# Unshifted exponentials with a checked range and a second, shifted program behind a branch; finishing in steps, like work kept together, B further ahead

## The chip, the cores and the metric

One core of a Trainium2 chip. Times are device microseconds (us) of a whole execution; most executions of one kernel agree within 0.3%. All runs told here were in the fast, undisturbed state, and each was timed beside runs of the kernel before on the same chip. The granted clock is the share of TensorE's full clock that the trace records, as a mean over the run.

## The reference, cut to what matters

Two independent blocks share the kernel: A, an attention over all 2,048 positions, and B, a causal attention in four segments of 512 with a memory carried from one segment to the next. Both have 32 heads of 32 columns. Their outputs stand side by side.

```python
# A
scores = einsum('bhqd,bhkd->bhqk', q, k) * 32 ** -0.5
o_A    = softmax(scores) @ v                  # 32 heads, 2048 x 2048
out_A  = o_A @ wo
# B, for each of four segments
p      = softmax(qs @ ks.T * scale + mask)    # 512 x 512, causal
a_mem  = (phi(qs) @ M) / (phi(qs) @ z + 1e-6)
o      = g * a_mem + (1 - g) * (p @ vs)
M, z   = M + phi(ks).T @ vs, z + phi(ks).sum()
out_B  = o @ wo
```

With the inputs given, scores are small: sums of 2,048 exponentials are near 2,048, so a softmax without a shift is safe here. Nothing guarantees that for other inputs.

## The kernel before

A Python planner writes the program: it keeps a simple clock for every engine, decides what TensorE does next, and records the operations. Each engine gets its list in the order recorded, and semaphores hold an operation back until what it needs is done.

Four heads are packed into the 128 rows of TensorE for the scores and into its columns for the value products. An A unit is four heads and 256 queries; a B item is four heads and one segment. TensorE writes its results to PSUM, and the probabilities go from there through a ring of 20 slots in SBUF. The main parts, with cuts marked `# ...`:

```python
SLOTS = [(0, 1, 2), (3, 4)]      # PSUM banks of the scores, used by turns
RING, HIGH = 20, 12

# scores and exponential: 3 banks, then 2
R.op("PE", f, ..., w=[("ps", bk) for bk in banks[:n]], mode="R")      # tiled by rows
cb, ck = self.cbA[b][:, k:k + 1], ("cbA", b, k)                       # B: cbB
R.op("ACT", lambda e: e.activation(self.PT[:, s0:s0 + n, 0:width], self.ps[...],
                                   ACTF.Exp, bias=cb, scale=SCALE), ..., cost=0.171 + n * width * 0.000833)

# the shift (B; A's is alike): squares, sums of squares, maximum over columns, over partitions
for k in range(2):
    R.op("DVE", lambda e, k=k: e.tensor_tensor(self.SQB[k][:, :], KQ[:, k, :], KQ[:, k, :], ALU.mult), ...)
R.op("PE", ...)                                    # 4 matmuls with blk32
yield from self.col_max(bank, 1, -SCALE, self.cbB[b][:, 0:1], ("cbB", b))   # reduce, diagonal, matmul, reduce
self.events.add(("sB", n))                         # only now may B's scores start

# value products and sums of one unit end: copy PSUM, then finish
R.op("DVE", lambda e: e.tensor_copy(self.OL[x][:, :], self.ps[:, OLB, :]), ...)
for q in range(2):                                 # finish()
    R.op("DVE", lambda e, Lq=Lq: e.reciprocal(Lq, Lq), ...)           # 128 columns each
    yield ("dve",)
R.op("DVE", lambda e: e.tensor_tensor(self.OTA[...], O, L, ALU.mult), ...)  # ...

# A or B next
it = b if b.kn < a.kn / 2 + LEAD else a            # LEAD = 3

# the planner's loop, when no scores can be put down now
full = len(self.ring_busy) > HIGH
for what in (("pv", "side") if full else ("side", "pv")):
    # "pv": a value product, if its exponentials are done
    # "side": projections, the memory, output projections, in chunks of up to 8 matmuls
```

## Time and profile before

| | before |
|---|---|
| median time (3 runs) | 1349.19 us (1347.47 to 1351.28) |
| score exponentials | 992, holding ScalarE 1,156 us |
| ScalarE's work, all activations (estimate from starts) | 1,191 us |
| ScalarE idle: first 160 us, middle, end | 67, 35, 58 us |
| TensorE's work (estimate, corrected below) | 1,203 us |
| changes of TensorE's tiling | 2,240 |

How the estimates are made: an activation's record is longer than what it holds of its engine, so I take starts. After an exponential of 1,024 elements the next one starts 996 ns later when nothing is waited for (median), after 1,536 elements 1,423 ns: 0.833 ns per element plus 143 ns. What lies beyond that between two starts is idle; a wait counts where it ends.

The head of the profile's page: busy time, share and count of each engine.

```profile
span 1350.1 us, 37376 instructions
PE 1232.8 (91%) x16968; PEld 509.2 (38%) x17194; DVE 831.7 (62%) x1391; ACT 1206.6 (89%) x1037; POOL 113.9 (8%) x207
```

The view of the waits from 140 to 1280 us (who waited <- for whom: us in total, times, longest):

```profile
ACT PT L471 <- PE ps L454: 16.8, 21, 3.8
```

In that stretch ScalarE hardly waits. The timeline shows what follows it (start, us, engine, line, operation, count, [idle before <- releaser]):

```profile
1268.84 7.42 ACT L471 ACTIVATE PT<-ps,cbA 128x1536 bf16<-128x1536 f32 x6 [0.62 <-PE ps L454]
1280.69 5.24 ACT L471 ACTIVATE PT<-ps,cbB 128x1536 bf16<-128x1536 f32 x5 [4.43 <-PE ps L454]
1285.80 0.65 ACT L762 ACTIVATE E<-KQB 128x512 bf16<-128x512 bf16 x1
1318.01 5.25 ACT L471 ACTIVATE PT<-ps,cbB 128x1024 bf16<-128x1024 f32 x5 [31.56 <-PE ps L454]
...
1331.17 15.48 PE L594 MATMUL ps<-WoB,OTB 128*128 128x512 bf16 x62 [5.91 <-DVE OTB L565]
```

The last B item comes 31.56 us late, and B's last output projection then runs alone.

### The profile page before, as it was taken

The page shows a single profiled execution, that of the slowest core. Times are in us where ns is not written, and L with a number is a line of the kernel's source. Part 1 is how long each engine was busy: PE and PEld are TensorE (multiplying, and loading weights), DVE is VectorE, ACT ScalarE, POOL GpSimd, SP SyncE. Part 2 cuts the span into 40 slices and gives each one's busy share as a digit, 9 for nine tenths or more (in the row PEclk, how much of TensorE's full clock was granted, in tenths as well). Part 3 has the DMA queues.
Part 4 walks back from the last instruction along what each step waited for, and adds up shares of the span by engine and source line. Part 5 has one row for each costly group of instructions (what it writes and reads, how often), then busy time and mean ns, then how long its engine had stood idle before and what let it go on. Part 6 is the DMA issues. An engine that isn't in the chain of part 4 may idle for free.

```text
span 1350.1 us, 37376 instructions
## 1 busy us (share of the span) xinstructions
PE 1232.8 (91%) x16968; PEld 509.2 (38%) x17194; DVE 831.7 (62%) x1391; ACT 1206.6 (89%) x1037; POOL 113.9 (8%) x207
## 2 busy tenths in 40 slices
PE   6788999999999988999899999999998999999996
PEld 3433343333333333333333333333333333333442
DVE  3665456555675567656647754757566675567674
ACT  3358989999999999999999999999999999999811
POOL 1000000100011011101100010111011111011110
PEclk9889999999999998999999999999998999999998
DMA  7325122311211122112211112111210113111111
GB/s 211 63 59 130 25 41 62 74 37 25 64 37 33 21 56 37 29 29 60 49 40 30 33 25 58 31 37 30 49 32 21 37 29 96 44 30 43 53 59 47
DMA packets 195870, 66.39 MB, mean 49 GB/s; under 512 B 187008, under 2 KB 187008, under 8 KB 195712
## 3 DMA queue, kind: packets, MB, share of 16 engines
q1 hardware_dynamic: 195712, 63.99, 20.2%
q8 instruction: 135, 2.21, 0.7%
q14 instruction: 23, 0.19, 0.0%
HBM read 40.90 MB, written 8.39 MB: 37 GB/s over the span
## 4 chain that ended last, share of the span: by engine, by line
ACT 66%; PE 23%; DVE 5%; SPq 2%; DMA 2%; issue 1%; POOL 0%; DVEq 0%
ACT PT L471 65%; PE ps L594 13%; PE ps L454 5%; PE ps L520 5%; DVE OL L540 2%; SPq L335 2%; ACT E L762 1%; DVE OL L530 1%; DMA PKt<-PH 1%; DVE outsb L837 1%; DMA WB<-in_B_wk_dram 0%; DMA out_dram<-outsb 0%; SPq L305 0%; DVE SQB L604 0%; DVE KQB L604 0%
## 5 line engine op out<-in xcount | busy, mean ns | idle before, releaser
L471 ACT ACTIVATE PT<-ps,cbA 128x1024 bf16<-128x1024 f32 (+1 forms) x832 | 1013.1, 1365 | 25.1 <-PE ps L454 24.6
L454 PE MATMUL ps<-QA,KA 32*128 32x256 bf16 x4096 | 328.7, 275 | 32.3 <-ACT PT L471 21.0
L520 PE MATMUL ps<-PT,ones 128*32 128x256 bf16 (+1 forms) x4864 | 315.0, 274 | 0.0
L520 PE MATMUL ps<-PT,VA 128*32 128x256 bf16 x4096 | 274.7, 282 | 1.5 <-DVE OL L530 0.8
L540 DVE RECIPROCAL OL<-OL 128x128 f32<-128x128 f32 x256 | 242.3, 948 | 5.2
L471 ACT ACTIVATE PT<-ps,cbB 128x768 bf16<-128x768 f32 (+3 forms) x160 | 171.4, 1197 | 62.5 <-PE ps L454 61.5
L454 PEld LDWEIGHTS ps<-QA,KA 32*128 32x128 bf16 x4096 | 95.3, 92 | 302.3 <-ACT PT L471 249.9
L594 PE MATMUL ps<-xB,WB 128*128 128x512 bf16 x683 | 187.2, 393 | 23.6 <-issue 13.2
L594 PE MATMUL ps<-xA,WA 128*128 128x512 bf16 x679 | 181.0, 385 | 14.1 <-issue 12.7
L491 POOL TENSOR_SCALAR_AFFINE_SELECT PT<-PT 128x512 bf16<-128x512 bf16 (+2 forms) x143 | 83.8, 601 | 1097.7 <-ACT PT L471 1096.5
L520 PEld LDWEIGHTS ps<-PT,VA 128*32 128x32 bf16 x4096 | 107.9, 95 | 134.3 <-issue 125.7
L530 DVE COPY OL<-ps 128x512 f32<-128x512 f32 x128 | 86.6, 677 | 73.6 <-PE ps L520 73.2
L520 PEld LDWEIGHTS ps<-PT,ones 128*32 128x32 bf16 x4864 | 130.7, 97 | 2.7 <-issue 0.3
L594 PEld LDWEIGHTS ps<-xB,WB 128*128 128x128 bf16 x768 | 62.4, 99 | 97.2 <-issue 45.0
L594 PEld LDWEIGHTS ps<-xA,WA 128*128 128x128 bf16 x768 | 61.5, 98 | 84.8 <-issue 34.7
L788 DVE RECIPROCAL den<-den 128x128 f32<-128x128 f32 x96 | 91.1, 949 | 2.1
L604 DVE CAST KQB<-ps 128x512 bf16<-128x512 f32 x64 | 43.4, 679 | 70.8 <-PE ps L594 70.8
L594 PE MATMUL ps<-WoB,OTB 128*128 128x512 bf16 x237 | 62.5, 391 | 8.8 <-DVE OTB L565 5.9
L837 DVE CAST outsb<-ps 128x512 bf16<-128x512 f32 x64 | 43.2, 678 | 37.9 <-PE ps L594 32.4
L454 PE MATMUL ps<-KQB 32*128 32x256 bf16 (+1 forms) x768 | 58.3, 265 | 6.9 <-ACT PT L471 4.3
L604 DVE CAST VT<-ps 128x512 bf16<-128x512 f32 x32 | 21.8, 681 | 67.3 <-PE ps L594 67.3
L594 PE MATMUL ps<-xA,OTA 128*128 128x512 bf16 x242 | 58.6, 380 | 3.7 <-issue 2.0
(76 smaller groups left out, 677.7 us busy)
## 6 DMA issues: line engine op xcount, KB each, us to landing
WB<-in_B_wk_dram SPq DMA_DIRECT2D x32, 256.0 KB, 2.8
WB<-in_B_wq_dram SPq DMA_DIRECT2D x32, 256.0 KB, 2.9
WB<-in_B_wv_dram SPq DMA_DIRECT2D x32, 256.0 KB, 3.1
out_dram<-outsb SPq DMA_DIRECT2D x32, 256.0 KB, 2.0
WA<-in_A_wqkv_dram SPq DMA_DIRECT2D x24, 256.0 KB, 3.6
OTA<-in_A_x_dram SPq DMA_DIRECT2D x16, 256.0 KB, 5.2
WoB<-in_B_wo_dram SPq DMA_DIRECT2D x1, 2048.0 KB, 9.8
xA<-in_A_wo_dram SPq DMA_DIRECT2D x1, 2048.0 KB, 9.4
```

What stands on the lines that cost most here:

```text
L335: R.dma(lambda e: e.dma_start(dst, src), w=keys, issue=0.5)
L454: ins = e.matmul(o, l, r, start=True, stop=True)
L471: op = R.op("ACT", lambda e: e.activation(self.PT[:, s0:s0 + n, 0:width], self.ps[:, banks[0]:banks[0] + n, 0:width], ACTF.Exp, bias=cb, s ...
L491: mo = R.op("POOL", lambda e, ap=ap, pat=pat: e.affine_select(ap, ap, pattern=pat, compare_op=ALU.is_ge, fill=0.0, base=0, channel_multipl ...
L520: ins = e.matmul(o, l, r, start=start, stop=end, skip_group_check=True)
L530: R.op("DVE", lambda e: e.tensor_copy(self.OL[x][:, :], self.ps[:, OLB, :]), r=[("ps", OLB)], w=[("OL", x)], cost=0.66)
L540: R.op("DVE", lambda e, Lq=Lq: e.reciprocal(Lq, Lq), r=[k], w=[k], cost=0.87)
L594: ins = e.matmul(o, l, rh, start=a, stop=z)
L604: op = self.R.op("DVE", lambda e: e.tensor_copy(dst, self.ps[:, bank, :]), r=[("ps", bank)], w=[dkey], cost=0.66)
L762: ex = R.op("ACT", lambda e: e.activation(self.E[:, k0:k1, :], KQ[:, k0:k1, :], ACTF.Exp), r=[("KQB", b, k) for k in range(k0, k1)], w=["E ...
L788: R.op("DVE", lambda e, cs=cs: e.reciprocal(self.den[:, cs], self.den[:, cs]), r=["den"], w=["den"], cost=0.9)
L837: op = R.op("DVE", lambda e, ns=ns, bank=bank, ob=ob: e.tensor_copy(self.outsb[ob][:, ns], self.ps[:, bank, :]), r=[("ps", bank)], w=[("ou ...
```

## The change

Its intent: exponentials without a shift, so that the bias is an immediate and the shift's work goes; a check on VectorE that sums and their reciprocals are in range, and the old, shifted program behind a branch if they aren't; the division split into steps between which other VectorE work may pass; TensorE stays with one kind of work once it has begun it; B is let further ahead of A.

```diff
-            cb, ck = self.cbA[b][:, k:k + 1], ("cbA", b, k)
+        cb, ck = 0.0, []                    # a pointer only if self.shifted
-                  cost=0.171 + n * width * 0.000833)
+                  cost=(0.171 if self.shifted else 0.085) + n * width * 0.000833)
@@ finish: a "dve" step before each reciprocal, and the check
-            R.op("DVE", lambda e, Lq=Lq: e.reciprocal(Lq, Lq), r=[k], w=[k], cost=0.87)
             yield ("dve",)
+            R.op("DVE", lambda e, cs=cs: e.reciprocal(rec[:, cs], L[:, cs]), r=[ko], w=[k], cost=0.93)
+        yield ("dve",)
+            R.op("DVE", lambda e: e.scalar_tensor_tensor(L, L, 1.0, rec, ALU.mult, ALU.add,
+                 accum_out=self.rng[:, u.seq:u.seq + 1]), ...)
@@ the shift: a_norm, total and B's part
+        if not self.shifted:
+            return
@@ pick
-            it = b if b.kn < a.kn / 2 + LEAD else a
+            it = b if b.kn < a.kn * SLOPE + LEAD else a        # SLOPE = 0.55
@@ the planner's loop
-            for what in (("pv", "side") if full else ("side", "pv")):
+            first = self.run if STICK and self.run else ("pv" if full else "side")
+            for what in (first, "side" if first == "pv" else "pv"):
...
+                if done:
+                    self.run = what                            # set to None by the next scores
@@ the end of each engine's program
+                eng.wait_ge(fast.sem["DVE"], fast.count[flag])
+                eng.reg_load(reg, self.flag[0:1, 0:1])
+                with eng.If_ne(reg, 0):
+                    fast.wait_all(eng)
+                    slow.play(eng, name)
```

Cut from it: the recorder's split into two programs, names of semaphores, the reduction of `rng` to one flag, a regrouping of scores that is switched off (`GROUP = 1`), the finishing tasks' higher priority, and a planned wait of a unit's first value product for the copy out of PSUM before it.

## The prediction

> **What bounds it now.** The groups view gives 992 score exponentials (PSUM to PT). In the timeline, starts of consecutive ones lie 996 ns apart after 1,024 elements and 1,423 after 1,536: 0.833 ns per element plus 143 ns. 1,216,512 elements and 992 instructions make 1,014 + 142 = 1,156 us; other activations add about 35. From 140 to 1280 us ScalarE waits for scores 16.8 us in all (view of the waits): it bounds that stage. The rest is a start of 140 us, where TensorE projects group 0 and ScalarE idles some 60 us, and a tail of 64 us after 1286 us: ScalarE waits 31.6 us for the last B item, then the last B output projection runs alone (62 matmuls recorded, 15.5 us).
>
> TensorE is close behind. From the starts of consecutive matmuls I estimate 1,160 us of work, 2,240 tiling changes at about 95 ns included, and 186 us of slack: 8 to 9% in the middle.
>
> **What changes.**
> 1. The bias becomes an immediate. The E exponentials have one already (reading SBUF) and hold ScalarE for stream + 93 ns. The Trainium skill, "ScalarE: Activation LUTs", section "What ACT_TABLE_LOAD costs", puts a [128,1] pointer operand at about 93 ns; no immediate exponential from PSUM is in the trace, so 143 - 93 = 50 ns is an estimate. Saved: 992 x 93 ns = 92 us, 80 of it where ScalarE bounds.
> 2. The shift's work goes: 64 + 128 square-sum and 51 diagonal matmuls (about 24 us of TensorE, plus some 18 us of tiling changes, estimated); on VectorE about 110 us.
> 3. Added on VectorE: 128 range checks of 256 float32; the like operation took 472 ns, so about 60 us. VectorE's total falls by 50 us (62% busy now, not binding).
> 4. Like work together: of 312 changes between value and full-array matmuls perhaps 120 vanish: 11 us of TensorE.
> 5. B ahead (0.55 for 0.5): B ends some six A units earlier. Each last A unit leaves TensorE about 5 us (estimate: 14.3 of ScalarE against 9 of TensorE), into which output projections fit: tail 64 to 25-35 us.
> 6. Finishing in steps lets evictions in between two reciprocals of 0.95 us: a few us at most.
> 7. At the end a reduction, a matmul, a register load and a jump over the second program: +5 us. Sums are near 2,048, so the flag stays 0.
>
> **Sum.** ScalarE's need: 1,190 - 92 = 1,098 us; TensorE's: 1,160 - 53 = 1,107: co-bound. ScalarE's idle time, 160 us now: start 85 to about 70 (no norm chain before the first scores), middle 17-25 to 28 (mutual waiting), tail 60 to about 28, end check 5. 1,098 + 70 + 28 + 28 + 5 = 1,229 us; predicted 1,228, range 1,192 to 1,260. Chances: faster by over 2% 0.97, within 0.02, slower 0.01.
>
> **What would show it.** (1) Exponentials start stream + 50 ns apart; if 90, the saving is half. (2) No square or diagonal matmuls, VectorE busy about 780 us. (3) Under 2,000 tiling changes; ScalarE's waits for scores in the middle grow from 17 to 30-50 us, TensorE's slack falls to 4-6%. (4) The last exponential is an A one, 25-35 us before the end. (5) About 5 us between last output and end.
>
> **What would make it wrong.** PSUM exponentials not gaining 93 ns (about 1,270); TensorE so full that preparation and output projections pile up at the end (1,250 or more); its granted clock (0.973 now) falling; VectorE queueing that holds PSUM; or a set flag, which runs everything twice.

## More of the kernel before

Groups by line and shape (line, engine, operation, tiles, shapes, count | busy us, mean ns | idle before, releaser):

```profile
L471 ACT ACTIVATE PT<-ps,cbA 128x1536 bf16<-128x1536 f32 x384 | 612.5, 1595 | 22.2 <-PE ps L454 22.1
L471 ACT ACTIVATE PT<-ps,cbA 128x1024 bf16<-128x1024 f32 x448 | 516.1, 1169 | 3.0 <-PE ps L454 2.5
...
L594 PE MATMUL ps<-xB,WB 128*128 128x512 bf16 x683 | 187.2, 393 | 23.6 <-issue 13.2 <-DMA WB<-in_B_wv_dram 4.3 <-DMA WB<-in_B_wk_dram 1.3
...
L594 PEld LDWEIGHTS ps<-xB,WB 128*128 128x128 bf16 x768 | 62.4, 99 | 97.2 <-issue 45.0 <-DMA WB<-in_B_wv_dram 4.8 <-DMA WB<-in_B_wk_dram 1.2
```

The first two lines are most of ScalarE's time; both read the bias from a tile (`cbA`). The last two hold a trap that I fell into: 768 weight loads, but 683 matmuls of the same line. The 85 others ran; they have no record. I come back to it.

"Middle" runs from 160 us to 30 us before the last exponential ends. TensorE's work is the time between its first and last matmul, less what the gaps between starts exceed the shortest gap of their kind by; it is good to some ten us.

## The result, and the profile after

The ratio of two kernels is the mean time of one's fast runs over that of the other's in the same rounds, so not quite the ratio of the medians quoted. Differences in us between kernels of different rounds are differences of such ratios times 1,350. The kernel before has a fourth run here, so its median differs from the one above.

| | before | after | predicted |
|---|---|---|---|
| median time | 1350.14 us | 1267.91 us (1265.81 to 1268.64) | 1228 (1192 to 1260) |
| ratio | 1 | 0.9391 (0.9372 to 0.9410) | |
| ScalarE's work | 1,191 us | 1,098 us | 1,098 us |
| ScalarE idle, first 160 us | 67 us | 71 us | 85 to 70 us |
| ScalarE idle, middle | 35 us | 59 us | 17-25 to 28 us |
| ScalarE idle, end (with the flag) | 58 us | 39 us | 60 to 33 us |
| TensorE's work, records corrected | 1,203 us | 1,161 us | 1,160 to 1,107 us |
| changes of tiling | 2,240 | 2,026 | under 2,000 |
| granted TensorE clock | 0.973 | 0.974 | |

The kernel became faster by 6.1%, 82 us, where 121 were predicted, and lies outside the range. Work and idle add up: 1,098 + 71 + 59 + 39 = 1,267 us. The prediction divided the 160 us of idle time before in another way (85, 17-25, 60) than the cuts used here do (67, 35, 58), so changes are safer to compare than levels: the start was to lose 15 us and gained 4, the middle was to gain 3 to 11 and gained 24, the end was to lose 27 and lost 19.

The page's head, and the groups:

```profile
span 1266.5 us, 36893 instructions
PE 1178.2 (93%) x16735; PEld 507.2 (40%) x16955; DVE 793.5 (63%) x1358; ACT 1119.8 (88%) x1037; POOL 115.1 (9%) x211
```

```profile
L532 ACT ACTIVATE PT<-ps 128x1536 bf16<-128x1536 f32 x416 | 625.7, 1504 | 47.6 <-PE ps L505 46.5
L532 ACT ACTIVATE PT<-ps 128x1024 bf16<-128x1024 f32 x480 | 508.3, 1081 | 16.1 <-PE ps L505 15.9
L674 PE MATMUL ps<-xB,WB 128*128 128x512 bf16 x696 | 186.9, 385 | 14.8 <-issue 10.2 <-DMA WB<-in_B_wv_dram 3.5 <-DMA WB<-in_B_wk_dram 0.4
...
L608 DVE SCALAR_TENSOR_TENSOR OL<-OL,SQ 128x256 f32<-128x256 f32 x128 | 57.4, 448 | 3.1
...
L608 DVE DVE_READ_ACCUMULATOR OL<-OL,SQ 128x1 f32 x128 | 10.4, 81 | 0.0
```

The tile `cbA` is gone from the exponentials, and the idle time before them is larger. By starts, 1,024 elements now hold ScalarE for 903 ns and 1,536 for 1,330: 93 ns less each, and the overhead is 50 ns. The two last lines are the range check.

The view of the waits, 140 to 1200 us:

```profile
ACT PT L532 <- PE ps L505: 23.3, 26, 4.6
ACT E L849 <- DVE KQB L684: 16.3, 4, 6.5
```

The second line is new: the exponential E of B's memory sits at the head of ScalarE's list and waits for a projection. The timeline shows two such places, and the end:

```profile
61.58 9.15 ACT L532 ACTIVATE PT<-ps 128x1536 bf16<-128x1536 f32 x8 [4.64 <-PE ps L505]
71.84 0.63 ACT L849 ACTIVATE E<-KQB 128x512 bf16<-128x512 bf16 x1 [1.11 <-DVE KQB L684]
91.53 9.55 ACT L532 ACTIVATE PT<-ps 128x1536 bf16<-128x1536 f32 x9 [19.06 <-PE ps L505]
...
71.22 8.81 PE L674 MATMUL ps<-xA,WA 128*128 128x512 bf16 x39
79.86 3.62 PE L674 MATMUL ps<-xB,WB 128*128 128x512 bf16 x16
83.31 3.62 PE L674 MATMUL ps<-xA,WA 128*128 128x512 bf16 x16
86.77 3.62 PE L674 MATMUL ps<-xB,WB 128*128 128x512 bf16 x15
...
1109.64 14.08 ACT L532 ACTIVATE PT<-ps 128x1152 bf16<-128x1152 f32 x14
1130.23 0.63 ACT L849 ACTIVATE E<-KQB 128x512 bf16<-128x512 bf16 x1 [6.52 <-DVE KQB L684]
1135.47 5.97 ACT L532 ACTIVATE PT<-ps 128x1536 bf16<-128x1536 f32 x5 [4.60 <-PE ps L505]
...
1207.66 20.94 ACT L532 ACTIVATE PT<-ps 128x1024 bf16<-128x1024 f32 x19 [0.63 <-PE ps L505]
...
1259.81 0.69 DVE L924 CAST outsb<-ps 128x512 bf16<-128x512 f32 x1 [1.04 <-PE ps L674]
1260.41 0.28 DVE L644 TENSOR_REDUCE gcol<-SQB 128x1 f32<-128x128 f32 x1
...
1261.15 0.16 DVE L650 TENSOR_SCALAR flag<-ps 128x1 int32<-128x1 f32 x1 [0.27 <-PE ps L648]
```

From 72 to 91 us ScalarE has nothing to do for 19.06 us. TensorE isn't idle: it runs projections and nothing else. The planner's own record of that stretch (the kernel's Python code run without the chip, its choices printed) says why:

```
planner's clock 70.85 to 87.89 us: ring 20 of 20 slots taken, so no scores;
the next value product is ready; chosen each time: "side", since "side" was the last kind
```

Value products alone free the ring, and only new scores make the planner forget its last kind. Once side work has begun with the ring full, it goes on until there is none left. The four waits of E, from 523 to 1130 us, are of the same kind: E belongs to side work, and at all four the planner's record again shows no room for scores, a value product ready (after the first chunk of side work), and "side" chosen since it was the last kind. The wait for the last B item is gone: the last 19 exponentials (1207.66) run in one piece, then output projections fill the end. From VectorE's last instruction to the end it is 5.2 us (2.7 before).

### The profile page after: what moved, and what is told of

Same layout as the page of the kernel before. It is cut to its first block, busy times and chain, and to the rows that moved or that the text cites. A ratio compares the mean times of both kernels' runs of the same rounds, so it can differ in the third digit from the quotient of the medians.

```text
span 1266.5 us, 36893 instructions
## 1 busy us (share of the span) xinstructions
PE 1178.2 (93%) x16735; PEld 507.2 (40%) x16955; DVE 793.5 (63%) x1358; ACT 1119.8 (88%) x1037; POOL 115.1 (9%) x211
## 4 chain that ended last, share of the span: by engine, by line
ACT 58%; PE 34%; DVE 3%; DMA 2%; SPq 1%; issue 1%; DVEq 0%; ACTq 0%
ACT PT L532 57%; PE ps L674 18%; PE ps L505 8%; PE ps L581 8%; SPq L384 1%; ACT E L849 1%; DMA PKt<-PH 1%; DVE SQ L604 1%; DMA WB<-in_B_wv_dram 1%; DMA WB<-in_B_wk_dram 0%; DVE OL L591 0%; DVE SQB L684 0%; DVE outsb L924 0%; PE ps L897 0%; DVE OL L608 0%
## 5 line engine op out<-in xcount | busy, mean ns | idle before, releaser
L532 ACT ACTIVATE PT<-ps 128x1536 bf16<-128x1536 f32 (+3 forms) x992 | 1088.5, 1247 | 65.9 <-PE ps L505 64.5
L581 PE MATMUL ps<-PT,ones 128*32 128x256 bf16 (+1 forms) x4864 | 304.0, 274 | 0.0
L581 PE MATMUL ps<-PT,VA 128*32 128x256 bf16 x4096 | 260.8, 279 | 1.3 <-DVE OL L591 1.2
L604 DVE RECIPROCAL SQ<-OL 128x128 f32<-128x128 f32 x256 | 242.6, 948 | 4.9
L674 PE MATMUL ps<-xA,WA 128*128 128x512 bf16 x681 | 185.5, 387 | 16.5 <-issue 13.6
L552 POOL TENSOR_SCALAR_AFFINE_SELECT PT<-PT 128x256 bf16<-128x256 bf16 (+2 forms) x147 | 84.8, 594 | 872.8 <-ACT PT L532 872.7
L608 DVE SCALAR_TENSOR_TENSOR OL<-OL,SQ 128x256 f32<-128x256 f32 x128 | 57.4, 448 | 3.1
```

The source lines that it names most:

```text
L532: op = R.op("ACT", lambda e: e.activation(self.PT[:, s0:s0 + n, 0:width], self.ps[:, banks[0]:banks[0] + n, 0:width], ACTF.Exp, bias=cb, s ...
L552: mo = R.op("POOL", lambda e, ap=ap, pat=pat: e.affine_select(ap, ap, pattern=pat, compare_op=ALU.is_ge, fill=0.0, base=0, channel_multipl ...
L581: ins = e.matmul(o, l, r, start=start, stop=end, skip_group_check=True)
L604: R.op("DVE", lambda e, cs=cs: e.reciprocal(rec[:, cs], L[:, cs]), r=[ko], w=[k], cost=0.93)
L608: R.op("DVE", lambda e: e.scalar_tensor_tensor(L, L, 1.0, rec, ALU.mult, ALU.add, accum_out=self.rng[:, u.seq:u.seq + 1]), r=[k, ko], w=[k ...
L674: ins = e.matmul(o, l, rh, start=a, stop=z)
```

## The experiments

Five ideas are tested: that TensorE's work now sets the pace (T), that ScalarE still does and is starved by the order (S, R, N), that VectorE does (V), that the two take turns (K, the corner), and that what the others leave doesn't depend on the order (W). C, Z, O and N2 are rivals named with their runs. "The order kept" means that no engine's list changes except for the instructions altered.

### mm7: less work for TensorE

```diff
-        mms = [(self.ps[:, bank, :], W[:, i, :], xsl(i), i == 0, i == NI - 1) for i in range(NI)]
+        mms = [(...) if self.shifted or i != 1 else None for i in range(NI)]   # None: planned, not issued
```

> The changed kernel with one of the eight matmuls of each of the 192 projections left out, the instruction order of every engine kept (wrong result on purpose). It takes 192 x 216 ns = 41 us from TensorE and nothing from the others. Theory T (after the change TensorE, which holds about 40 us more work than I counted since some 190 full-array matmuls have no record in the trace, sets the pace of the middle): 25 to 40 us faster than the changed kernel, 1228 to 1243. Rival S (ScalarE still bounds and is only starved by a few accidents of the order): at most 10 us faster. Rival V (VectorE, with its new range checks, holds the others up): at most 10 us faster.

Measured 1255.56 us (1254.72 to 1256.68), ratio 0.9296: 13 us faster than the changed kernel; the result wrong. T fails: a third of the 41 us shows. It is also a little more than the 10 us that S and V allowed. The estimate of TensorE's work fell by 43 us, so the cut was made.

### act_cut: less work for ScalarE

```diff
 # shortened; a memset at the start sets the columns left out to one
-  e.activation(self.PT[:, s0:s0 + n, 0:width], self.ps[..., 0:width], ACTF.Exp, ...)
+  e.activation(self.PT[:, s0:s0 + n, 0:width - 32], self.ps[..., 0:width - 32], ACTF.Exp, ...)
```

> The changed kernel with each score exponential 32 columns narrower in each of its slots, the order kept (wrong result on purpose; the columns left out are set to one at the start). It takes 2,432 slots x 32 x 0.833 ns = 65 us from ScalarE and nothing from TensorE. T: at most 20 us faster than the changed kernel (1248 or more). S: 45 to 65 us faster (1203 to 1223). V: at most 10 us.

Measured 1238.66 us (1236.77 to 1240.25), ratio 0.9164: 31 us faster. (A one in place of an exponential near one is within the tolerance.) Neither T's 20 nor S's 45: ScalarE counts for about half.

### ptr_bias: the pointer back

```diff
+        self.zb = sb("zb", [P, 1], F32)              # set to zero once
-        cb, ck = 0.0, []
+        cb, ck = self.zb[:, 0:1], ["zb"]
```

> The changed kernel with the bias read from a [128,1] column of zeros in place of the immediate; the order kept, the result unchanged. It gives ScalarE its 992 x 93 ns = 92 us back. Starts of two exponentials 996 and 1,423 ns apart again. T: 40 to 75 us slower than the changed kernel (ScalarE has to catch up with TensorE before it bounds again). S: 85 to 95 us slower.

Measured 1348.71 us (1345.63 to 1350.11), ratio 0.9981 to before. The pointer costs 80 of its 92 us, between T's 75 and S's 85, and with it the changed kernel is level with before: 0.2%, inside the interval of 0.9951 to 1.0012. Starts were 996 and 1,423 ns apart again.

### no_check: the range check almost gone

```diff
-  e.scalar_tensor_tensor(L, L, 1.0, rec, ALU.mult, ALU.add, accum_out=self.rng[:, u.seq:u.seq + 1])
+  e.tensor_copy(self.rng[:, u.seq:u.seq + 1], L[:, 0:1])
```

> The changed kernel with each range check (about 424 ns and an accumulator read of 81 ns) replaced by a copy of one column; order, flag and branch kept. It takes about 50 us from VectorE. V: 15 us or more faster. T and S: within 5 us of the changed kernel.

Measured 1268.89 us (1266.47 to 1271.22), ratio 0.9391, that of the changed kernel. VectorE's busy time fell by 36 us (793.5 to 757.3, not the 50 I gave), and nothing came of it. V fails.

### imm_only: the immediate alone, in the kernel before

```diff
-                                                ACTF.Exp, bias=cb, scale=SCALE),
+                                                ACTF.Exp, bias=0.0, scale=SCALE),
```

> The kernel before with nothing changed but the operand: the bias of the score exponentials is the immediate zero; the shift is still computed and waited for, the order kept, the result unchanged. Theory R (the gain of the change is the pointer's 92 us alone; the rest of it nets zero, because stretches in which side work stays first while the probability ring is full starve ScalarE for as long as the shift's removal and the shorter tail save): 75 to 90 us faster than before, 1262 to 1275, so level with the changed kernel within 1%. Rival C (TensorE's work is what limits both, and the removal of the shift's matmuls was needed to cash in the pointer): at most 60 us faster, 1290 or more.

Measured 1313.55 us (1310.04 to 1316.19), ratio 0.9724: 37 us, not 75 to 90. R fails here: the immediate alone isn't the gain. C's bound of 60 us holds. With `ptr_bias` this makes a square (ratios times 1,350):

| | pointer | immediate | gain |
|---|---|---|---|
| program before | 1350 us | 1313 us | 37 us |
| program after | 1347 us | 1268 us | 80 us |

The program's change is worth nothing while the pointer is there, and 45 us without it. The waits of this kernel, 140 to 1240 us, and its groups:

```profile
ACT PT L471 <- PE ps L454: 36.5, 75, 4.7
```

```profile
L594 PE MATMUL ps<-xB,WB 128*128 128x512 bf16 x768 | 206.9, 393 | 8.0 <-DMA WB<-in_B_wv_dram 2.2 <-DMA WB<-in_B_wk_dram 1.6 <-DVE KQB L604 1.1
```

75 waits in place of 21, many of them short. And this trace has all 768 matmuls of the line: the 85 were in before's program too.

### stick_release and no_stick: the rule about like work

```diff
 # stick_release
+            blocked = cur is not None and not self.ring_room([min(len(x), left) for x in use])
-            first = self.run if STICK and self.run else ("pv" if full else "side")
+            first = self.run if STICK and self.run and not blocked else ("pv" if full else "side")
 # no_stick
-STICK = True
+STICK = False
```

> The changed kernel, with the last kind of side work no longer kept first when the next scores find no room in the ring (one condition added). R: the stall of 19 us near 91 us and the four waits of the E exponential for KQB (16 us in all) vanish or shrink to a third, and the time falls by 15 to 40 us, to 1228 to 1252. C: the side work has to be done anyhow and its time comes back elsewhere as waits of ScalarE for scores; within 8 us of the changed kernel.

> The changed kernel with the keeping together of like work switched off. Tiling changes rise from 2,026 by 100 to 250. R: ScalarE's stalls with a full ring go, the added changes cost TensorE up to 24 us of which a third shows: 0 to 25 us faster than the changed kernel. C: slower by 5 to 20 us, since TensorE has more to do.

`stick_release`: 1275.82 us (1268.81 to 1281.03), ratio 0.9429 (0.9384 to 0.9475), 5 us slower than the changed kernel, which lies inside the two intervals. `no_stick`: 1269.45 us (1266.93 to 1270.07), ratio 0.9388, the same; its tiling changes rose to 2,191. In both the stall of 19 us went and ScalarE's idle time at the start fell from 71 to 56 and 52 us; the waits of E in the middle went too, and the long waits there fell from 36 to 27 and 25 us. But the last B item came late again. ScalarE's timeline of `stick_release`:

```profile
1212.18 0.63 ACT L849 ACTIVATE E<-KQB 128x512 bf16<-128x512 bf16 x1 [15.30 <-DVE KQB L684]
1236.33 4.85 ACT L532 ACTIVATE PT<-ps 128x1024 bf16<-128x1024 f32 x5 [23.51 <-PE ps L505]
```

The idle time at the end is 74 and 71 us in place of 39. What the stalls had cost came back at the end: as C had it for `stick_release`, while for `no_stick` the slowdown that C gave didn't come either.

### slope50: B's lead as before

```diff
-SLOPE = 0.55
+SLOPE = 0.5
```

> The changed kernel with B's lead as before (0.5 for 0.55). If B running ahead shortens the tail by the 20 us that the two traces differ by, the time from the last exponential and its last wait to the end grows from 38 us back to 45 to 60 us and the kernel is 8 to 20 us slower. If the order of the middle decides instead, the difference has either sign and the waits in the middle show it.

Measured 1283.23 us (1281.53 to 1286.19), ratio 0.9489: 13 us slower. The wait of 31 us for the last B item is back and the idle time at the end is 64 us. Since the whole order is planned anew, the 13 us aren't the lead's alone; the clock was lower too (0.964 to 0.970, against 0.974 to 0.979).

### both_cut: less work for both

> Both cuts in one kernel: one of eight projection matmuls left out (41 us less of TensorE; alone 12 us faster) and exponentials 32 columns narrower (65 us less of ScalarE; alone 29 us faster); order kept, wrong result on purpose. Theory K (the changed kernel sits on the corner where TensorE and ScalarE bind by turns): more than the sum of the two, 48 to 65 us faster than the changed kernel, 1203 to 1220. Rival O (fixed waits of the order, the same for any speed of the two): the sum or less, 1227 or more.

The edits of `mm7` and `act_cut` together. Measured 1215.19 us (1211.75 to 1216.19), ratio 0.9003: 52 us faster than the changed kernel, and 9 us more than the 13 + 31 of the parts; from the four intervals that 9 is uncertain by about 7. So K is favoured, not by much: where one engine is relieved, the other takes its place. Yet of 106 us taken out half doesn't show.

### keep_shift and noshift: what the shift's work is worth

```diff
 # keep_shift: the changed kernel, the shift computed but not used
-        if not self.shifted:
-            return
 #   also, for lack of memory: the reciprocal in place, the check one column
 # noshift: the kernel before, immediate bias, a_norm, total and B's part removed, "sB" set at once
```

> The changed kernel with the shift still computed and waited for but not used (square sums, maxima, diagonals; the range check cut to one column since the memory for both is lacking, which cost nothing in its own run). K: TensorE gets about 45 us back and the first scores wait for the chain again: 25 to 60 us slower than the changed kernel, 1293 to 1328. Rival Z (the shift's removal is worth nothing, as the changed kernel with the pointer put back, level with before, might suggest): within 10 us of the changed kernel.

> The kernel before with the immediate bias and without the shift's work; no range check, no second program, the old finishing, the old order rules. K: the 38 us of the immediate alone grow to 60 to 80, since TensorE is relieved as well: 1270 to 1290. Z: within 10 us of the immediate alone (1303 to 1323).

`keep_shift`: 1335.12 us (1332.67 to 1336.75), ratio 0.9891, 67 us slower, more than either theory gave. `noshift`: 1282.55 us (1280.16 to 1287.37), ratio 0.9519, 28 us faster than `imm_only`. Z fails in both. By the estimate the shift's work is some 24 us of TensorE in both pairs (1,161 to 1,185; 1,202 to 1,179), so the 67 us are not that work alone: in `keep_shift` ScalarE waits for scores 114 us from 140 to 1300 us. How much of it is the chain's waiting and how much an unlucky order or the reciprocal in place isn't told apart.

```profile
ACT PT L531 <- PE ps L504: 114.2, 26, 32.6
```

### finish_old: finishing in one piece

```diff
-            self.spawn(self.finish(u), (-2, u.seq), f"fin{u.seq}")
+            self.spawn(self.finish(u), -1, f"fin{u.seq}")
-            yield ("dve",)
             R.op("DVE", lambda e, cs=cs: e.reciprocal(rec[:, cs], L[:, cs]), ...)
+            yield ("dve",)
-        yield ("dve",)
```

> The changed kernel with the finishing as before: the first reciprocal put down at once, the division right after the second, and the old priority. If finishing in steps matters, VectorE's evictions come late and the kernel is 5 to 20 us slower; if not, within 5 us either way.

Measured 1283.94 us (1280.28 to 1286.16), ratio 0.9509: 16 us slower. The order changes with it, so this too is the step together with its order, and with a lower clock (0.966 to 0.974).

### tuned and tuned_stick: another order

```diff
+            # tuned: stick_release's condition; tuned_stick: without it
-SLACK, PACE = 0.25, 200
+SLACK, PACE = 0.15, 150
-                  cost=(0.171 if self.shifted else 0.085) + n * width * 0.000833)
+                  cost=(0.171 if self.shifted else 0.045) + n * width * 0.000833)
```

> A version meant to beat both kernels at the same work of every engine: the changed kernel with three things of its order altered: the last kind of work is no longer kept first while the next scores find no room in the ring; the order is planned with the overhead of an exponential nearer to the measured 50 ns (45 in place of 85); scores may come 0.1 us later and A's preparation sooner (0.15 for 0.25, 150 for 200). If order decides how much of the corner's waiting is left (theory N), 15 to 35 us faster than the changed kernel, 1233 to 1253, with no wait of over 10 us between 100 us and the last exponential. If the work of TensorE and ScalarE sets the time whatever the order (theory W), within 8 us of it.

> The same as the run tuned but with like work kept together also while the ring is full, as in the changed kernel. N: slower than tuned by 10 to 30 us, with the stall of some 19 us before 100 us and waits of the E exponential for KQB back. W: within 8 us of tuned.

`tuned`: 1268.28 us (1267.50 to 1270.98), ratio 0.9402, level with the changed kernel (W). `tuned_stick`: 1306.32 us (1305.93 to 1307.59), ratio 0.9680, 38 us slower, with a stall of 19 us before 91 us and one of 29 us at the end (N, and more than its 10 to 30). Each theory is right about one: with one planning the rule costs nothing, with another 38 us.

### no_branch: the second program

```diff
-            for shifted in (False, True):
+            for shifted in (False,):              # and no register load, no branch
```

> The changed kernel without the second program and the branch (the range check and its flag are still computed): 1 to 4 us faster than the changed kernel; the time from the last instruction of VectorE to the end falls from 5.2 us to 2 to 4 us. Should it be over 10 us faster, the second program costs more than the end of the trace shows.

Measured 1263.61 us (1262.73 to 1264.85), ratio 0.9361: 4 us faster. Its timeline ends:

```profile
1258.53 0.69 DVE L916 CAST outsb<-ps 128x512 bf16<-128x512 f32 x1 [1.03 <-PE ps L666]
...
1259.88 0.16 DVE L642 TENSOR_SCALAR flag<-ps 128x1 int32<-128x1 f32 x1 [0.27 <-PE ps L640]
```

1.9 us later the span (1261.9 us) is over, against 5.2 us with the branch: 3.3 of the 4 us are the end, and the second program costs next to nothing before it.

### tuned_mm7 and tuned_act_cut: the cuts again, in that order

> The run tuned with one of eight projection matmuls left out (41 us less of TensorE; wrong result on purpose; order kept). In the changed kernel the same cut gave 12 us. Theory W (with the stalls of the full ring gone, TensorE's work sets the time): 25 to 40 us faster than tuned, 1228 to 1243. Rival N2 (tuned is held by waits of its order as much as the changed kernel): 15 us or less.

> The run tuned with exponentials 32 columns narrower per slot (65 us less of ScalarE; order kept, columns left out set to one at the start). In the changed kernel the same cut gave 29 us. W: at most 20 us faster than tuned. N2: 25 to 45 us faster.

`tuned_mm7`: 1259.33 us (1257.88 to 1260.25), ratio 0.9322, 11 us faster than `tuned`; `tuned_act_cut`: 1229.18 us (1227.91 to 1231.85), ratio 0.9103, 40 us faster. W, that TensorE's work sets the time of `tuned`, is refuted: ScalarE counts for more, as in the changed kernel, and both numbers are within what N2 gave. A caution: with the order kept, work taken out early can't draw in work from the end. The time from the last exponential to the end stayed at 38 to 45 us in all five kernels with a cut. So these runs measure who binds where, not what a new plan could make of the room.

### order2: one more order

```diff
+            # stick_release's condition
-SLACK, HIGH, PACE, LEAD, SLOPE = 0.25, 12, 200, 3, 0.55
+SLACK, HIGH, PACE, LEAD, SLOPE = 0.05, 11, 180, 2, 0.7
-                  cost=(0.171 if self.shifted else 0.085) + n * width * 0.000833)
+                  cost=(0.171 if self.shifted else 0.080) + n * width * 0.000833)
```

> A second version meant to beat both kernels, again at the same work of every engine: like work is not kept first while the next scores find no room in the ring, B runs further ahead (0.7, lead 2), scores may come 0.2 us later, the ring counts as full from 11 on, A's preparation is paced at 180, an exponential is planned with 80 ns of overhead. If what is left of the miss is order (long waits of ScalarE in the middle, 36 us in the changed kernel and 37 in tuned, and a tail of 38 us), a better order shows it: 8 to 20 us faster than the changed kernel, 1248 to 1260, ScalarE's waits of over 1 us in the middle under 25 us in sum. If the changed kernel's time is the floor of this work, within 8 us of it.

Measured 1261.81 us (1258.96 to 1263.13), ratio 0.9348 (0.9317 to 0.9379): 6 us faster than the changed kernel and the fastest with the right result, the check and the branch, but the two intervals touch. That is under the 8 to 20 us that a better order was to show, though the long waits of the middle fell to 15 us as asked. The timeline near the end of its exponentials:

```profile
1198.11 1.02 ACT L532 ACTIVATE PT<-ps 128x1024 bf16<-128x1024 f32 x1 [0.23 <-PE ps L505]
1205.14 5.07 ACT L532 ACTIVATE PT<-ps 128x1024 bf16<-128x1024 f32 x5 [6.01 <-PE ps L505]
```

They are done at 1210 us, 18 us sooner than in the changed kernel (1229), but the rest takes 51 us in place of 38. Most of the 18 us comes back.

## Why the prediction was wrong, point by point

ScalarE's waits, from the starts, tell the story of the middle:

| kernel | ratio | waits of 20 ns to 1 us, middle | waits over 1 us, middle | idle at the start | idle at the end | TensorE's clock halved, whole run |
|---|---|---|---|---|---|---|
| before | 1 | 17 us | 7, 16 us | 67 us | 58 us | 72 us |
| imm_only | 0.9724 | 62 us | 6, 15 us | 69 us | 60 us | 55 us |
| noshift | 0.9519 | 63 us | 10, 14 us | 60 us | 40 us | 83 us |
| ptr_bias | 0.9981 | 14 us | 13, 33 us | 69 us | 39 us | 74 us |
| after | 0.9391 | 21 us | 15, 36 us | 71 us | 39 us | 67 us |
| stick_release | 0.9429 | 19 us | 11, 27 us | 56 us | 74 us | 57 us |
| no_stick | 0.9388 | 20 us | 13, 25 us | 52 us | 71 us | 36 us |
| tuned | 0.9402 | 19 us | 17, 37 us | 53 us | 59 us | 32 us |
| order2 | 0.9348 | 27 us | 7, 15 us | 61 us | 58 us | 42 us |

- **The immediate (item 1) was right to the nanosecond.** 93 ns less per exponential, an overhead of 50 ns, ScalarE's work 1,098 us as predicted. The figure of the Trainium skill, "ScalarE: Activation LUTs", section "What ACT_TABLE_LOAD costs" (about 93 ns for a [128,1] pointer operand), agrees with this trace: 996 - 903 and 1,423 - 1,330 ns. That 80 of the 92 us shorten the run, as item 1 has it, is met in the changed program; in the old one it is 37.
- **The shift's removal and the tiling (items 2 and 4) relieved TensorE by about 42 us, not 53.** The shift is worth some 24 us of the 42 I gave, its tiling changes included (76 fewer in `noshift`); the other 138 of the 214 changes that went are 13 us at about 95 ns each. Item 4's size was about right: `no_stick` has 165 changes more, 16 us, where 120 and 11 us were given. The Trainium skill, "TensorEngine Tiling (Array Packing)", section "Key Properties", says that changing the tiling mode drains TensorE; the trace fits that, with some 95 ns beyond the stream at each change (311 in place of 215 ns after 512 columns).
- **VectorE (items 3 and 6).** It doesn't bind, as predicted (`no_check`); its busy time fell from 832 to 794 us, where 780 were predicted. Undoing the finishing in steps, with the order that follows from it, costs 16 us: more than the few I gave it.
- **The tail (items 5 and 7) was nearly right.** Idle time at the end 58 to 39 us, 33 predicted; the last exponential is one of A, 38 us before the end; flag and branch cost 4 us (`no_branch`), 5 predicted, and the check nothing that shows (`no_check`). But item 5 was right partly by luck: the four orders without the rule's hold on the full ring have a lead of 0.55 or more too, and 58 to 74 us idle at the end. So the lead alone doesn't make the short tail of the changed kernel; that its stalls, in which side work gets done early, are the other half is argued.
- **The start failed.** 15 us less idle were predicted and 4 more came. The first exponential does start 5 us sooner (18.1 against 23.2 us), as the missing norm chain should make it, but a stall of 19 us follows at 72 us, from the rule that keeps like work together. The three orders without that rule's hold on the full ring, and the one without the rule, start with 52 to 61 us idle: there the gain is to be seen.
- **The middle failed, and is the larger part.** 28 us of "mutual waiting" stood in the sum; 59 came. By the table, the short waits are 21 us, and 62 us in `imm_only`; that they are few because the new plan expects shorter exponentials is argued, since no run changed that number alone. What wasn't foreseen are 15 waits of over 1 us, 36 us together: four of E (17 us), one right behind the last of them (5 us), six that begin or end while TensorE ran at half its clock (8 us, see below), and four others (7 us). The first five are no lack of capacity: with the pointer back, when TensorE has by the estimate some 180 us of slack, they are still there, and 12 of its 13 long waits come at the same exponentials.

The steps that failed are the sum's "middle 17-25 to 28 (mutual waiting)" and its "start 85 to about 70", and behind both item 4, "Like work together: of 312 changes ... perhaps 120 vanish: 11 us of TensorE". I counted that rule as a saving and not as a rule that holds value products back while the ring is full. In the trace this hold is a stall of 19 us at the start and 22 us of waits at and behind E in the middle, and both are gone in `no_stick`.

There is one thing that I overlooked. The trace records TensorE's granted clock, and it isn't evenly 0.974: it is 1, and 0.5 in stretches of 3.4 to 13.7 us. The matmuls confirm it: those of 512 columns start 427 ns apart in such a stretch, 216 ns elsewhere. The view by windows (us, then busy us of PE, PEld, DVE, ACT, POOL, then the clock, DMA share and GB/s) shows one of them and the stretch behind it:

```profile
233.60:247.20 13.60, 13.27 (x133) 3.98 (x125) 10.36 (x15) 10.98 (x11) 2.63 (x5) 0.50 0.01 3
247.40:261.00 13.60, 13.03 (x207) 5.71 (x204) 5.53 (x11) 13.50 (x13) 0.00 (x0) 1.00 0.00 1
```

TensorE is as busy in both, but has 133 matmul records in place of 207, and ScalarE is busy for 10.98 us in place of 13.50. In the middle of the changed kernel the clock is halved for 44 us, and 11 of ScalarE's 59 idle us lie in them; before, it is 48 us and 10 of 35. So the clock doesn't explain why the middle grew, but about 22 us (half of the 44, an estimate) of what I counted as TensorE's slack there were not to be had. It also blurs comparisons of orders: `tuned` ran at 0.986, `slope50` at 0.964 to 0.970, and `stick_release` took 1281.03 us at 0.973 and 1268.81 at 0.984. What in an order brings the halving on isn't known.

And the stalls are not 36 + 19 us that could simply be had, so they don't by themselves explain the 39 us that the prediction missed. Every order that took the stall away got most of it back at the end: ScalarE's idle time in all is 169 us in the changed kernel, 170 in `no_stick`, 178 in `stick_release`, 169 in `tuned` and 163 in `order2` (and 186, 187 and 206 in `finish_old`, `slope50` and `tuned_stick`). During a stall TensorE works off side work; in these orders about as much idle time was then missing at the end. That ties in with a second mis-sized term: TensorE's need. I gave 1,107 us, 9 more than ScalarE's; measured are 1,161, 63 more. Of the difference 45 us are matmuls without a record (1,841 records of 2,048 full-array matmuls of the projections before; 207 x 216 ns), the rest the items above. The page showed it: 683 matmuls on 768 weight loads. With the right number the middle's slack is 5 to 6%, not 8 to 9%, and little room in which side work could vanish.

What stays open: why none of eight orders has less than 163 us of idle time, where the prediction needed 131. That it is TensorE's total work, or that work with its halved clock, is argued, not shown; the cuts of TensorE's work alone gave only a third or less, and they can't settle it since they kept the order. Also open is how much of the 67 us of `keep_shift` is the order.

## What to carry to other kernels

Two engines that are both nine tenths full need not give up all of a saving on one of them: here 93 ns off each exponential were worth 37 us in one program and 80 in the other, out of 92. Before counting slack on an engine, compare counts of records with counts that the program fixes (weight loads against matmuls), and subtract what has no record. And a rule that saves switches must not outlive the moment when the other kind of work is what the bottleneck waits for; but look at the end of the timeline before calling a stall a loss, since work moved out of it has to be done somewhere. Look at the clock slice by slice, too, before a wait is put down to the order.

## What the Trainium skill lacked or had wrong

- "ScalarE: Activation LUTs", section "What ACT_TABLE_LOAD costs": its 186 ns + 0.833 N with immediates, less an overlap of about 93 ns back to back, leaves 93 ns of overhead, and no source is named. Here that holds for SBUF alone (E, 946 ns for 1,024 elements); reading PSUM it is 50 ns (after, 903 ns for 1,024). "Perfetto Trace Analysis", section "Optimizing Scalar/DVE Operations", tells the two apart (about 93 and 51 ns) and agrees. The first page's 93 ns for a pointer operand is right.
- "Perfetto Trace Analysis": I found no word there on matmuls without a record. Before, 1,841 of the 2,048 full-array projection matmuls have one (10% lack one); `imm_only`, `no_stick` and `tuned` have all 2,048.
- "TensorEngine Tiling (Array Packing)": it says that a change of mode drains TensorE but gives no time; here about 95 ns beyond the stream, 2,026 to 2,240 times.
- Ending on a flag: "Advanced Engine Details and Errata" has times for single branches, but I found no page with the cost of the whole; a wait for the flag, a register load on each engine and a jump over a second program cost 4 us here (`no_branch`).
